# Two products' copies put ahead of both exponentials, and a third product given another bank

## The chip, the cores and the metric

The kernel runs on one core of a Trainium2 chip. Five engines of that core work side by side, each through its own instructions in order: TensorE (PE, matrix products; its weight loads are listed apart as PEld), VectorE (DVE), ScalarE (ACT), GpSimd (POOL) and SyncE (SP), which here only starts transfers. They wait for one another through semaphores. Matrix products land in PSUM, an accumulator memory that is used here as eight banks of 128 partitions by 512 floats; the other engines copy from there to SBUF, the main on-chip memory. The metric is device time in microseconds, lower is better.

## The reference

A batch of attention heads, where each query row keeps only its 32 highest scores, is followed by a two-layer network with an exact GELU:

```python
scores = (q @ k.T) / sqrt(64)                # 8 batches, 8 heads, 576 rows of 64
kth = 32nd largest score of each row
attn = softmax(where(scores >= kth, scores, -1e9))
x = (attn @ v), heads side by side           # 4608 rows of 512
h = x @ w_in                                 # 512 -> 2048
g = 0.5 * h * (1 + erf(h / sqrt(2)))
out = g @ w_out                              # 2048 -> 512
```

All of it is in 32-bit floats.

## The kernel before, in words

The attention is cut into 144 items, 18 for each batch. A main item is a pair of heads and a tile of 128 query rows; the last 64 query rows of a batch (row tile `NM`) make two more items, each with two pairs of heads. In an even batch the sixteen main items come first and the two of the last rows after them, in an odd batch the other way round. Two batches make a ring of 36 items (`RINGS`), and "item 5 of a ring" means an item whose number is 5 modulo 36. Main items come in twos, and the product with the values is done at the odd one of the two, for both.

One pass of the main loop, number n, works on several items at once: scores of item n+2 (`scores`, and `last_keys` for their last keys), the 32 highest of item n (`top_k` on DVE, helped by sums on POOL), threshold and exponentials of item n-1 (`threshold` on POOL; `select` and `softmax` on ACT), the transposes of item n-2 (`transposes`), and the product of item n-3 (`attend`). Between these the loop puts pieces of the two-layer network, `mlp(1)`, so that PE has work. The order written in the loop is the order on each engine; no planner changes it.

`softmax(n - 1, e)` issues the exponential of one of two heads on ACT and adds up its denominators. From these, POOL (`add_small`, line 547) and DVE (`inverse`, the reciprocal of line 541) make the factor with which POOL normalises the row (line 589). The GELU and the exponential need different tables of ACT, so a pass has table loads.

Some items are transposed in another way: DVE turns blocks of 32 by 32 (`square_p`), SP writes them to DRAM (`write_p`, line 632) and reads them back turned into the tile `pt` (`read_p`, line 642). For those the product comes a pass later. `moved(i)` says so of main items: items 3, 5, 13, 23, 25 and 31 of a ring (`LATER`), from item 36 on and only below 136. `delayed(i)` says so of items of the last query rows: 16, 18 and 19 of a ring. Their product is not done at the usual place of the pass, but in `mids`, which calls `attend`, then copies the product into `xT` (`copy_x`), the input of the network, and then starts the next reads into `pt`.

Where in an odd pass `mids` stands is set here (`room` counts network pieces, `mid` lists products to do, `starts_next` holds the second item of each batch, among them item 19 of a ring):

```python
if mid and (mid[0] in starts_next or mid[0] % RINGS == LATER[0]):
    mlp(1); mids()
softmax(n - 1, 0)
if mid:
    mlp(1); mids()
if n % 2 and ahead_of_x:
    softmax(n - 1, 1)
```

`LATER[0]` is 3. So for item 3 and for item 19 the product and its copy are issued ahead of both exponentials, for the other moved items between the two, or behind the first where the second comes later in the pass.

PSUM is shared out by tags. From pass 13 on (`few`), `bank(name)` always gives the one bank `z`: it serves the product `seven` of the network (`seven_piece`, copied out as `p` at line 1003), the small transposes `tp_t` with the last keys of a later item (copied out at 381 and 677), and products `o` that are not moved. `pair_tile(name)` gives the two banks `pr`: for the scores `s_ps` (copied out at 416), for the transposes `tp` (lines 688 and 703), and for a moved item's product `o`, which takes one of the two. In an even pass the scores of two items are made, the first of them in the two banks `l1`, which also hold the network's first layer `h_ps`. A new user of a tag waits until the last one has been copied out.

Of the kernel before, what the change touches and what calls it, by code (L numbers as in the profile page):

```python
# [14 lines left out]
def kernel(  # L15
# [76 lines left out]
    def raw_of(n, pair):  # L92
        if n != "v":
            return raws[n][pair % 2 if pair < SQUARES else 0]
        return raws[n][pair % len(raws[n])]
# [7 lines left out]
    def issue(f):  # L103

        if held[0]:
            late_issues.append(f)
        else:
            f()
# [8 lines left out]
    def load(n, pair, queue=None, queue2=None):  # L117
        if pair >= n_pairs:
            return
        queue = queue or nc.sync  # L120
        queue2 = queue2 or queue
        b, h0 = pair // NP, 2 * (pair % NP)
        src = sources[n]
        if n != "v" and pair >= SQUARES:
            t = flat[n][0]
            for e in range(2):
                at = e * TL if n == "k" else 0
                for d in range(2):
                    rows, cols = slice((2 * e + d) * SQ, (2 * e + d + 1) * SQ), slice(d * SQ, (d + 1) * SQ)
                    queue.dma_start(  # L130
                        out=t[rows, at : at + S].rearrange("i (c j) -> i c j", j=SQ),
                        in_=src[b, h0 + e, :, cols].rearrange("(c i) j -> i c j", i=SQ),
                    )
            return
        t = raw_of(n, pair)
        for e in range(2):

            end = TL if pair >= SQUARES and e == 0 else S
            main = end % S
            queue.dma_start(  # L140
                out=t[:, 0:NM, e, :], in_=src[b, h0 + e, main : main + SM].rearrange("(t p) d -> p t d", p=P)
            )
            rows = slice(0, TL) if n == "q" else slice(e * TL, (e + 1) * TL)
            queue2.dma_start(out=t[rows, NM, e, :], in_=src[b, h0 + e, end - TL : end])
# [121 lines left out]
    def place_of(b, row):  # L266

        if row < SM:
            return b // 2 * RING + b % 2 * (SM + 2 * TL) + row
        return b // 2 * RING + SM + b % 2 * TL + row - SM  # L270
# [9 lines left out]
    def bank(name):  # L280

        tag = "z" if few[0] else ("z", "y0", "y1", "y2")[turn[0] % 4]
        turn[0] += 1
        return ps.tile([P, 512], f32, tag=tag, bufs=1, name=name)
# [75 lines left out]
    def half(r, e):  # L360


        return slice((r ^ e) * TL, ((r ^ e) + 1) * TL)

    def pair_tile(name, tag="pr"):
        return ps.tile([P, 2, 512], f32, tag=tag, bufs=1, name=name)
# [114 lines left out]
    def smaller(i):  # L481

        if paired(i):
            both, top = lists_of[i][:, :, 1].bitcast(i32), lists_of[i][:, :, 0].bitcast(i32)
            nc.gpsimd.tensor_tensor(into_of(i)[:, :, 1].bitcast(i32), both, top, op=ALU.subtract)  # L485
# [73 lines left out]
    def softmax(i, e):  # L559

        if i < 0 or i >= N:
            return
        st, s = stat_of[i], row(i, e)
        if (i, e) not in selected:
            select(i, e)
        nc.scalar.activation(  # L566
            s, s, func=AF.Exp, bias=st["bias"][:, e : e + 1], scale=1.0,
            accum_out=st["den"][:, e : e + 1],
        )
# [23 lines left out]
    def squared(i):  # L593

        if not SINGLE.stop - 2 < i < N - 2:
            return False
        if items[i][1] == NM:
            return i % RINGS != RINGS // 2 - 1
        return moved(i) or (i % 2 == 0 and i % RINGS != 12)

    LATE = (15, 17, 19, 23)
    LATER = (3, 5, 13, 23, 25, 31)

    def moved(i):

        return RINGS <= i < N - 8 and i % RINGS in LATER

    def delayed(i):

        return squared(i) and items[i][1] == NM  # L610
# [4 lines left out]
    RINGS = 2 * len(items) // B  # L615
# [114 lines left out]
    shared = []  # L730

    def column(tok):

        at = tok % RING
        return at if at < COLS else at - COLS

    def attend(i):

        if i < 0 or i >= N:
            return False  # L740
        pair, t = items[i]
        b, at = divmod(pair, NP)
        if t < NM and t % 2 == 0:
            return False
        pt = pt_now[0]
        both = t == NM and delayed(i - 1) and not delayed(i)
        alone = t < NM or not delayed(i) or delayed(i ^ 1)
        o = shared.pop() if both else pair_tile("o")[:, 0] if moved(i) else bank("o")
        off = 2 * TL if both else 0
        n, row = (2 * P, (t - 1) * P) if t < NM else (TL, SM)  # L750
        tok = place_of(b, row)
        gap = RING if t == NM else COLS if tok % RING >= COLS else RING - COLS
        assert read[0] >= tok - gap + n
        c = slice(column(tok), column(tok) + n)
        if t < NM:
            vt = raw_of("v", pair)
            for j in range(NJ):
                for e in range(2):
                    nc.tensor.matmul(  # L759
                        o[e * D : (e + 1) * D, 0:n], lhsT=vt[:, j, e, :],  # L760
                        rhs=pt[:, e * NJ + j if j < NM else NM, :],
                        start=(j == 0), stop=(j == NJ - 1),
                    )
            copies.append(lambda: nc.scalar.copy(out=xT[:, at, c], in_=o[:, 0:n]))
        else:
            for r in range(2):
                vt = raw_of("v", pair + r)
                for j in range(NJ):
                    for e in range(2):
                        nc.tensor.matmul(  # L770
                            o[e * D : (e + 1) * D, off + r * TL : off + (r + 1) * TL],
                            lhsT=vt[:, j, e, :],
                            rhs=pt[:, e * NJ + j if j < NM else NM, i % 2 * P :][:, half(r, e)],
                            start=(j == 0), stop=(j == NJ - 1),
                        )
            if not alone:
                shared.append(o)
            else:
                first = 0 if both else at
                copies.append(lambda: nc.scalar.copy(  # L780
                    out=xT[:, first : at + 2, c],
                    in_=o[:, 0 : off + 2 * TL].rearrange("p (r n) -> p r n", n=TL),
                ))

        if t == (NM if b % 2 == 0 else NM - 1):
            for r in range(2 if t == NM else 1):
                f = lambda r=r: load("v", pair + r + NP)
                if delayed(i) or moved(i):
                    soon.insert(0, f)
                elif both and r:  # L790
                    later.append(f)
                else:
                    issue(f)
        if at == (NP - 1 if t < NM else NP - 2):
            assert n_tok[0] == tok
            n_tok[0] = tok + n
        return True
# [333 lines left out]
    def mlp(n):  # L1131
        for _ in range(n):
            if done[0] >= len(pieces) or pieces[done[0]][0] > ready[0] or left[0] == 0:
                return
            pieces[done[0]][1]()
            done[0] += 1
            left[0] -= 1
            if eager[0]:
                run_gelus()
                run_small(9)  # L1140
# [69 lines left out]
    starts_next = [x + 1 for x in starts]  # L1210
    sums_in = {START + 8 + j: j for j in range(FT // 2)}
    ahead = N + 4
    for n in range(ahead):

        held[0] = n < N and squared(n - 2)
        mid = [i for i in (n - 5, n - 4) if delayed(i) and n % 2 and (i % 2 or i in starts)]
        if moved(n - 4):
            mid = [n - 4]
# [9 lines left out]
        def mids():  # L1228
            attend(mid.pop(0))
            if not mid:  # L1230
                copy_x()
                read_p(n - 3)
                issue_soon()
# [66 lines left out]
            softmax(n - 1, 1)  # L1300
        if few[0]:
            room = ODD if n % 2 else 0
            if mid and (mid[0] in starts_next or mid[0] % RINGS == LATER[0]):
                mlp(1)
                mids()
                room -= 1
            if n % 2 or not ahead_of_x:
                softmax(n - 1, 0)
            if mid:
                mlp(1)  # L1310
                mids()
                room -= 1
            if n % 2 and ahead_of_x:
                softmax(n - 1, 1)
            mlp(room)
# [24 lines left out]
        if n > 0:  # L1340
            smaller(n + 1)
        late_exps = RINGS < n < N - 1 and n % RINGS in LATE
        if not late_exps:
# [93 lines left out]
```

## Time and profile before

| | |
|---|---|
| median of 3 runs | 1458.59 us (1458.47 to 1459.49) |
| the profiled execution's own time | 1461.52 us |
| its span, first to last instruction | 1459.6 us |
| mean granted clock of TensorE | 0.999 |
| ACT busy, with its share of the span | 1050.2 us, 72% |
| POOL busy | 1131.3 us, 78% |

The rows in the prediction are of three kinds. A row of waits gives the engine and line that waited, the engine, tile and line it waited for, and then the total, the number of times and the longest, in microseconds. A row of the order of time gives the start in microseconds from the start of the span, the duration, the engine, the line, the operation, the tile written and the tiles read, the shapes, and how many such instructions are put together; in brackets stands how long the engine was idle before it and what ended that. A row of a window gives its bounds, its length, and the busy time of PE, PEld, DVE, ACT and POOL in it with their numbers of instructions, then the clock, the share of the DMA engines and the rate of transfers. Ends of matmuls are modelled, because TensorE works on several at once.

### The profile page before, as it was taken

How to read it: one execution, taken by the hardware profiler on the slowest of the kernel's cores; microseconds unless marked ns; L12 is line 12 of the kernel's file. 1: busy time of each engine (PE TensorE's matmuls, PEld its weight loads, DVE VectorE, ACT ScalarE, POOL GpSimd, SP SyncE). 2: the span in 40 equal slices, each digit the busy share in tenths (PEclk: the TensorE clock that was granted, in tenths of full speed). 3: DMA queues.
4: the chain of work that ended last, by engine and by line, in shares of the span. 5: the costliest groups of instructions: out<-in, count | busy, mean ns of one | idle time of the engine just before them, and what ended most of it. 6: DMA issues, size and time to landing. Idle time of an engine off the chain costs nothing. (4 is left out here: it accounts for less than half of the span.)

```text
span 1459.6 us, 26560 instructions
## 1 busy us (share of the span) xinstructions
PE 1439.8 (99%) x8567; PEld 1121.3 (77%) x8567; DVE 1324.4 (91%) x3345; ACT 1050.2 (72%) x1871; POOL 1131.3 (78%) x1290
## 2 busy tenths in 40 slices
PE   8999999999999999999999999999999999999999
PEld 6776578877777778787777778778777777787887
DVE  8999899999999999999999999999999999999701
ACT  7999977767768776777776777777676767677620
POOL 6787657887798878887898878886888887878632
PEclk9999999999999999999999999999999999999999
DMA  7524310045465446556646365556556443664200
GB/s 199 147 87 119 91 48 1 9 100 100 92 135 97 83 90 145 106 121 130 121 88 129 64 121 105 128 115 128 115 104 138 90 80 78 133 125 92 50 15 15
DMA packets 627147, 143.57 MB, mean 98 GB/s; under 512 B 532768, under 2 KB 618560, under 8 KB 627008
## 3 DMA queue, kind: packets, MB, share of 16 engines
q1 hardware_dynamic: 625744, 141.45, 46.1%
q8 instruction: 68, 1.11, 0.3%
q14 instruction: 71, 0.58, 0.1%
q10 hardware_dynamic: 1200, 0.39, 0.1%
q0 software_dynamic: 64, 0.03, 0.0%
HBM read 88.73 MB, written 53.08 MB: 97 GB/s over the span
## 5 line engine op out<-in xcount | busy, mean ns | idle before, releaser
L828 PE MATMUL h_ps<-xT,w_in_sb 128*128 128x256 f32 (+1 forms) x2560 | 532.6, 361 | 0.0
L828 PEld LDWEIGHTS h_ps<-xT,w_in_sb 128*128 128x128 f32 x2560 | 439.6, 191 | 67.3 <-issue 10.9
L511 DVE MAX8 top<-lists 128x8 f32<-128x576 f32 (+1 forms) x792 | 474.8, 638 | 0.0
L589 POOL TENSOR_TENSOR s<-s,stat 128x1152 f32<-128x1152 f32 x135 | 311.2, 2305 | 30.9 <-DVE stat L541 29.9
L554 ACT ACTIVATE s<-s,stat 128x576 f32<-128x576 f32 x288 | 217.7, 778 | 127.1 <-POOL stat L534 126.9
L514 DVE MATCH_REPLACE8 lists<-top,lists 128x288 f32<-128x288 f32 (+1 forms) x528 | 307.4, 587 | 0.0
L566 ACT ACTIVATE s<-s,stat 128x576 f32<-128x576 f32 x288 | 224.0, 781 | 7.8
L477 POOL TENSOR_TENSOR lists<-s 128x576 int32<-128x576 int32 x133 | 189.5, 1425 | 0.0
L485 POOL TENSOR_TENSOR lists<-lists 128x576 int32<-128x576 int32 x132 | 186.1, 1410 | 3.1
L759 PE MATMUL o<-pt,raw_v 128*64 128x256 f32 x1280 | 153.0, 384 | 1.9 <-DMA pt<-turned 1.3
L416 ACT ACTIVATE s<-s_ps 128x1024 f32<-128x1024 f32 x127 | 124.8, 1030 | 32.6 <-PE s_ps L408 32.4
L759 PEld LDWEIGHTS o<-pt,raw_v 128*64 128x64 f32 x1280 | 87.3, 137 | 78.9 <-issue 34.4
L984 PE MATMUL y_ps<-w_out_sb,sum 128*128 128x256 f32 x472 | 140.5, 379 | 0.0
L547 POOL TENSOR_SCALAR stat<-stat 128x2 f32<-128x2 f32 x144 | 31.3, 217 | 136.1 <-ACT s L566 129.3
L408 PE MATMUL s_ps<-kt,qm 64*128 64x512 f32 x512 | 129.9, 620 | 0.8 <-ACT s L414 0.8
L844 ACT ACTIVATE g<-h_ps 128x512 f32<-128x512 f32 x144 | 78.2, 595 | 70.6 <-PE h_ps L828 70.1
L984 PE MATMUL y_ps<-w_out_sb,g 128*128 128x256 f32 x480 | 118.0, 383 | 0.0
L514 DVE MATCH_REPLACE8 lists<-first,lists 128x288 f32<-128x288 f32 x264 | 113.9, 436 | 0.0
L526 DVE MAX8 first<-lists 128x8 f32<-128x288 f32 x268 | 106.9, 438 | 0.0
L446 DVE TENSOR_TENSOR lists<-s 128x576 f32<-128x576 f32 x133 | 103.9, 781 | 2.1 <-ACT s L381 2.0
L984 PEld LDWEIGHTS y_ps<-w_out_sb,g 128*128 128x128 f32 x480 | 90.0, 190 | 16.9 <-issue 5.4
L622 DVE STREAM_TRANSPOSE s<-s 128x1152 f32<-128x1152 f32 x74 | 100.8, 1363 | 0.0
(162 smaller groups left out, 2315.6 us busy)
## 6 DMA issues: line engine op xcount, KB each, us to landing
turned<-s SPq DMA_DIRECT2D x296, 144.0 KB, 3.5
pt<-turned SPq DMA_DIRECT2D x296, 144.0 KB, 3.2
raw_v<-in_v_dram SPq DMA_DIRECT2D x64, 128.0 KB, 2.8
raw_q<-in_q_dram SPq DMA_DIRECT2D x112, 72.0 KB, 2.4
raw_k<-in_k_dram SPq DMA_DIRECT2D x112, 72.0 KB, 2.4
out_dram<-y SPq DMA_DIRECT2D x30, 256.0 KB, 3.5
w_out_sb<-in_moe_w_in_dram SPq DMA_DIRECT2D x14, 511.8 KB, 4.9
w_out_sb<-in_moe_w_out_dram SPq DMA_DIRECT2D x10, 511.8 KB, 4.1
```

The lines of the kernel that those rows point to most:

```text
L408: nc.tensor.matmul(s_ps[:, e], lhsT=q_t[rows, :], rhs=kt[rows, main_keys(pair)], start=True, stop=True)
L416: nc.scalar.activation(spread(s, S + TL, SM), s_ps, func=AF.Copy, scale=scale)
L477: nc.gpsimd.tensor_tensor(t[:, :, 1].bitcast(i32), a.bitcast(i32), b.bitcast(i32), op=ALU.add)
L485: nc.gpsimd.tensor_tensor(into_of(i)[:, :, 1].bitcast(i32), both, top, op=ALU.subtract)
L511: nc.vector.max(x[:, e], src[:, e])
L514: nc.vector.match_replace(dst[:, e], x[:, e], src[:, e], LOWEST)
L554: nc.scalar.activation(s, s, func=AF.Prelu, bias=st["neg"][:, e : e + 1], scale=1.0, alpha=STEEP)
L566: nc.scalar.activation(s, s, func=AF.Exp, bias=st["bias"][:, e : e + 1], scale=1.0, accum_out=st["den"][:, e : e + 1],)
L589: nc.gpsimd.tensor_tensor(s, s, wide, op=ALU.mult)
L759: nc.tensor.matmul(o[e * D : (e + 1) * D, 0:n], lhsT=vt[:, j, e, :], rhs=pt[:, e * NJ + j if j < NM else NM, :], start=(j == 0), stop=(j = ...
L828: nc.tensor.matmul(h_tile(u)[:, i, :], lhsT=w_in_sb[:, ko, f * P : (f + 1) * P], rhs=xT[:, ko, c0 : c0 + n], start=(ko == 0), stop=(ko == ...
L984: nc.tensor.matmul(acc[names][:, k], lhsT=lhsT, rhs=rhs, start=(j == 0 and k == 0), stop=(j == FT // 2 - 1 and k == 1),)
```

## The change

Two things are changed. The list of items whose product and copy are issued ahead of both exponentials grows from item 3 to items 3, 5 and 31 of a ring. By `moved`, this concerns items 41, 77 and 113, and items 67 and 103. And the product of item 19 of a ring, the last one of the last query rows (items 55, 91 and 127), takes one of the two banks `pr` in place of the bank `z`. `attend(18)`, just before it, keeps `z`. Nothing is computed differently.

```diff
     LATE = (15, 17, 19, 23)
+    COPY_FIRST = (3, 5, 31)
     LATER = (3, 5, 13, 23, 25, 31)
...
         alone = t < NM or not delayed(i) or delayed(i ^ 1)
-        o = shared.pop() if both else pair_tile("o")[:, 0] if moved(i) else bank("o")
+        aside = moved(i) or delayed(i) and i in starts_next
+        o = shared.pop() if both else pair_tile("o")[:, 0] if aside else bank("o")
...
             room = ODD if n % 2 else 0
-            if mid and (mid[0] in starts_next or mid[0] % RINGS == LATER[0]):
+            if mid and (mid[0] in starts_next or mid[0] % RINGS in COPY_FIRST):
                 mlp(1)
                 mids()
                 room -= 1
```

## The prediction

> **What bounds the kernel now.** I read the shares of the engines first, then what TensorE (PE) and VectorE (DVE) waited for, then the order of time around the three kinds of place that the change touches.
>
> ```profile
> span 1459.6 us, 26560 instructions
> ...
> PE 1439.8 (99%) x8567; PEld 1121.3 (77%) x8567; DVE 1324.4 (91%) x3345; ACT 1050.2 (72%) x1871; POOL 1131.3 (78%) x1290
> ```
>
> ```profile
> PE tp L688 <- ACT xT L764: 3.5, 4, 1.0
> ...
> PE o L759 <- DMA pt<-turned: 1.3, 1, 1.3
> ...
> PE o L770 <- ACT p L1003: 0.8, 3, 0.3
> ```
>
> ```profile
> DVE stat L541 <- POOL stat L547: 51.8, 54, 6.2
> ```
>
> ```profile
> 592.00:724.00 132.00, 131.90 (x752) 103.22 (x751) 129.71 (x328) 94.55 (x169) 105.12 (x118) 1.00 0.62 121
> ```
>
> The first view says that PE is busy for 99% of the span and DVE for 91%. The second (total, times, longest, in us) names nearly all that PE loses once the start is over: the transposes `tp` wait four times for the copy into `xT`, and the product `o` waits three times for the copy `p` out of the bank `seven`. Those seven waits, 4.3 us, are the whole prize. The third row shows that DVE waits for PE's side of the kernel too: 54 times for a GpSimd (POOL) result. The last row (length, then busy PE, weight loads, DVE, ACT, POOL) shows a stretch in which both are full: 131.9 and 129.7 of 132 us. So a microsecond given to PE counts only if DVE can follow, and I look for that at each place.
>
> The Trainium skill, "Perfetto Trace Analysis", section "Identifying the Most-Contended Engine", would have TensorE judged by its weight loads and not by matmul busy time; by that PE stands at 77%, DVE at 91% is the bound, and filling PE's gaps brings nothing. The rows bear on it so: 1121.3 us over 8567 loads is 0.13 us each, while four `seven` matmuls in the next fence take 0.215 us each from start to start (436.60 to 437.46), so a stretch without a gap shows loads well under 100% too. The kinds differ, so the trace does not settle it; a time in which PE's gaps bring nothing is the second rival.
>
> **The change part by part.** (a) Item 5 of a ring, three places (items 41, 77, 113). PE's, ACT's, POOL's and DVE's order of time at the first:
>
> ```profile
> 436.60 1.03 PE L982 MATMUL seven<-w_sum,g 128*128 128x256 f32 x4
> 437.46 1.03 PE L984 MATMUL y_ps<-w_out_sb,g 128*128 128x256 f32 x4
> 438.42 2.38 PE L759 MATMUL o<-pt,raw_v 128*64 128x256 f32 x20
> ...
> 443.45 0.59 PE L984 MATMUL y_ps<-w_out_sb,sum 128*128 128x256 f32 x2
> 445.02 1.09 PE L688 MATMUL tp<-ident,s 128*128 128x128 f32 x8 [0.97 <-ACT xT L764]
> ...
> 446.91 1.99 PE L408 MATMUL s_ps<-kt,qm 64*128 64x512 f32 x8
> 448.83 1.52 PE L759 MATMUL o<-pt,raw_v 128*64 128x256 f32 x12
> ```
>
> ```profile
> 442.15 0.38 ACT L1003 COPY p<-seven 128x256 f32<-128x256 f32 x1
> 442.55 1.28 ACT L566 ACT_TABLE_LOAD   x1
> 443.84 0.78 ACT L566 ACTIVATE s<-s,stat 128x576 f32<-128x576 f32 x1
> ...
> 444.62 0.35 ACT L764 COPY xT<-o 128x256 f32<-128x256 f32 x1
> 444.87 0.78 ACT L566 ACTIVATE s<-s,stat 128x576 f32<-128x576 f32 x1
> ...
> 445.64 0.26 ACT L381 ACTIVATE s<-tp_t 128x128 f32<-128x128 f32 x1
> 445.80 0.26 ACT L677 COPY pt<-tp_t 128x128 f32<-128x128 f32 x1
> 446.15 1.01 ACT L703 COPY pt<-tp 128x1024 f32<-128x1024 f32 x1
> ```
>
> ```profile
> 452.35 0.73 POOL L865 TENSOR_TENSOR sum<-g 128x256 f32<-128x256 f32 x1 [1.33 <-PE y_ps L984]
> ...
> 457.38 0.22 POOL L547 TENSOR_SCALAR stat<-stat 128x2 f32<-128x2 f32 x1
> ```
>
> ```profile
> 456.11 0.79 DVE L526 MAX8 first<-lists 128x8 f32<-128x288 f32 x2
> 457.63 0.17 DVE L541 RECIPROCAL stat<-stat 128x2 f32<-128x2 f32 x1 [0.74 <-POOL stat L547]
> ```
>
> The product `o` lies in the transposes' banks and ended at 438.42 + 2.38 = 440.80; its copy stood behind the table load (1.28) and the first exponential (0.78) and began at 444.62. Ahead of both it begins when L1003 ends, at 442.53, and is done by 442.88. PE's last matmul before the transposes ends at 444.04, so they start 0.97 earlier. On ACT nothing is added: the copy takes 0.25 (444.62 to 444.87) on either side of the exponential, the first exponential comes 0.25 later, the second, which ends the sums that POOL waits for, stays at 444.87. PE's order of work is the same, SP's and POOL's too: the multilayer piece and the `pt` read follow the product as before.
>
> What is late next: `pt<-tp` (L703) cannot start before L677 ends, 445.80 + 0.26 = 446.06, and holds the banks to 447.07. The second half of the scores `s_ps` needs them: the eight matmuls run from 446.91 to 448.83, 0.96 for half, so 0.97 earlier the half would start at 446.90. With some 0.05 for the signal (copy end 444.97 to transposes 445.02) it waits about 0.22: 0.75 is left. DVE's limit is the same by accident: POOL's run from 452.35 to 457.38 starts when PE has read the old sums, moves with PE, and DVE is ready at 456.90 against 457.63. I take 0.74 a place, 2.2 in all. Bounds: nothing (DVE or a DMA takes it) to 0.97 a place, 2.9.
>
> (b) Item 19, the last product of the last query rows, three places (55, 91, 127), first one:
>
> ```profile
> 574.78 1.39 PE L770 MATMUL o<-pt,raw_v 128*64 128x64 f32 x40 [0.26 <-ACT p L1003]
> ...
> 579.12 1.04 PE L688 MATMUL tp<-ident,s 128*128 128x128 f32 x8
> ```
>
> ```profile
> 576.24 0.27 ACT L780 COPY xT<-o 128x128 f32<-128x128 f32 x1 [1.51 <-PE o L770]
> ```
>
> ```profile
> 592.10 0.17 DVE L541 RECIPROCAL stat<-stat 128x2 f32<-128x2 f32 x1 [0.32 <-POOL stat L547]
> ```
>
> In the transposes' banks it no longer waits for `seven` to be copied out of the shared bank: 0.26 off. ACT stood idle 1.51 for this product, so its whole following chain moves with it. The new holder costs nothing: the next user of the banks is `tp` at 579.12 and the copy ends at 576.51, 2.6 before. DVE's wait of 0.32 at 592.10 lets 0.26 through. Matmul ends are modelled, so the true gap may be larger; DVE would pass 0.32 of it. I take 0.26 a place, 0.8 in all, bounds 0 and 1.0. Zero is the case where the next `pt` read sets the pace: PE waited 1.3 for one once.
>
> (c) Item 31, two places (67, 103; item 139 is past the last moved one):
>
> ```profile
> 687.38 2.38 PE L759 MATMUL o<-pt,raw_v 128*64 128x256 f32 x20
> ...
> 688.89 0.38 ACT L1003 COPY p<-seven 128x256 f32<-128x256 f32 x1
> ...
> 692.38 0.26 ACT L381 ACTIVATE s<-tp_t 128x128 f32<-128x128 f32 x1
> ...
> 692.57 0.22 POOL L547 TENSOR_SCALAR stat<-stat 128x2 f32<-128x2 f32 x1 [1.32 <-ACT s L566]
> 693.53 0.22 POOL L534 TENSOR_SCALAR stat<-top 128x2 f32<-128x2 f32 x1 [0.74 <-DVE top L511]
> ...
> 1035.25 1.09 PE L688 MATMUL tp<-ident,s 128*128 128x128 f32 x8 [0.53 <-ACT xT L764]
> 1066.67 0.17 DVE L541 RECIPROCAL stat<-stat 128x2 f32<-128x2 f32 x1 [1.14 <-POOL stat L547]
> ```
>
> At 67 there is no wait of PE to remove, and a wait is added: ACT is ready for the copy at 689.27, the product ends at 689.76, so ACT stands 0.49 with the table load, both exponentials and two copies behind it. The cover: POOL's sum L547 moves from 692.57 to 693.06, and POOL's next instruction waits for DVE until 693.53 anyway. Cost 0; without that cover it would be up to 0.5. At 103 PE's 0.53 goes, and DVE's next wait, 1.14, lets it through: 0.53. It may be less in a run where PE was not late there (the 1.3 us DMA wait stands before it in the same ring).
>
> Sum: 2.2 + 0.8 + 0.5 = 3.5 on the profiled execution, whose own time is 1461.5, its span 1459.6; it lies 2.9 above the median of 1458.6. Since (c) may be a loss of that execution alone, the timed runs should gain 3.0 to 3.5: 1458.6 - 3.3 = 1455.3.
>
> **The rivals.** *More.* If the banks are free in time and DVE follows fully: 3 x 0.97 + 3 x 0.32 + 0.53 = 4.4, time 1454.2. For it: the stalls repeat exactly and everything after them shifts alike. Against: 446.06 and 457.63 above both stop at 0.74.
>
> *It is taken back.* PE's gaps go, but DVE or the `pt` reads keep their times, as in the full stretch from 592 to 724; the second half of the ring absorbs it. Gain 0 to 0.8, time about 1458.2. For it: DVE's 129.71 of 132. Against: DVE waits before and after that stretch (0.74, 0.32, 1.14) for what PE delivers.
>
> *Slower.* DVE's L446 and POOL's L589 follow the same reciprocal, and once in the trace they met:
>
> ```profile
> 446.94 0.73 DVE L446 TENSOR_TENSOR lists<-s 128x576 f32<-128x576 f32 x1
> ...
> 1007.78 2.11 POOL L589 TENSOR_TENSOR s<-s,stat 128x1152 f32<-128x1152 f32 x1
> 1008.08 2.42 DVE L446 TENSOR_TENSOR lists<-s 128x576 f32<-128x576 f32 x1 [0.51 <-ACT s L381]
> ```
>
> There L446 waited 0.51 for ACT's L381, started behind L589 and took 2.42 for 0.73: 1.69 lost. If the reordered ACT queue makes L381 late at the five moved places, that is 8.4 against 3.5 gained: 1463.5. It decides when L381 ends after DVE reaches L446: 445.90 against 446.94 at item 5, which the change does not delay, and 692.64 + 0.49 = 693.13 at item 67, where DVE cannot start it before POOL's 693.53. Over 0.4 us of margin at all five, so unlikely. The Trainium skill, "SBUF - State Buffer", "Who interferes with whom", says that a DVE instruction with two SBUF inputs is blocked for a whole GpSimd instruction that reads SBUF; the 2.42 beside 2.11 agrees.
>
> **How the numbers follow.** Forecast 0.49 (its own range 1454.6 to 1456.2), more 0.20, taken back 0.24, slower 0.07. A measurement of this kernel tells about 0.2%, 2.9 us, from no change: faster means below 1455.7. Three quarters of the forecast and all of "more" lie there, 0.57; the rest of the forecast and "taken back" are no change, 0.36; slower 0.07. The range 1453.6 to 1458.6 takes in the first two and most of the third.
>
> **What would show it.** Right: in PE's waits `tp` for `xT` and `o` L770 for `p` are gone, scores L408 for `pt` L703 stand there with about 0.2 three times; ACT's copy lies ahead of the table load and waits 0.5 for PE at item 67; DVE's wait for L547 shrinks by about 3 us. Wrong: PE's waits gone but as much idle time in new rows (`pt<-turned`, h_ps, L703 with more than 0.7 each), or L446 with over 2 us at a changed place.

## The result and the profile after

The changed kernel takes 1455.88 us (median of 16 runs, 1455.24 to 1457.15) against 1458.72 (1458.40 to 1460.01), a ratio of 0.998 with a 95% interval of 0.9972 to 0.9987: 2.84 us less, where 3.3 were forecast. That is 0.19%, clear of the runs' spread and just on the no-change side of the 0.2% that the prediction had drawn. The profiled execution took 1455.84 us with a span of 1453.9.

What TensorE waits for in the changed kernel (total, times, longest), first its row of shares:

```profile
PE 1439.0 (99%) x8567; PEld 1117.4 (77%) x8567; DVE 1322.6 (91%) x3345; ACT 1049.8 (72%) x1871; POOL 1131.5 (78%) x1290
```

```profile
PE s_ps L408 <- ACT pt L704: 0.5, 3, 0.2
...
PE o L772 <- DMA pt<-turned: 0.3, 1, 0.3
```

The four waits of the transposes for `xT` and the three of the product for `p` are gone. In their stead stand three waits of the scores for the copy L704 (L703 before), 0.5 in all, and one for a read into `pt`. The shares hardly moved: they were no measure of what could be had. DVE's wait for POOL, 51.8 us before, is

```profile
DVE stat L541 <- POOL stat L547: 47.4, 48, 6.2
```

4.4 less, where about 3 was given as a sign.

At item 5, first place, in the order of time of PE, ACT and DVE:

```profile
441.86 0.59 PE L986 MATMUL y_ps<-w_out_sb,sum 128*128 128x256 f32 x2
442.30 1.04 PE L689 MATMUL tp<-ident,s 128*128 128x128 f32 x8
...
444.13 1.13 PE L408 MATMUL s_ps<-kt,qm 64*128 64x512 f32 x4
445.44 1.13 PE L408 MATMUL s_ps<-kt,qm 64*128 64x512 f32 x4 [0.18 <-ACT pt L704]
446.49 2.38 PE L761 MATMUL o<-pt,raw_v 128*64 128x256 f32 x20
```

```profile
440.56 0.38 ACT L1005 COPY p<-seven 128x256 f32<-128x256 f32 x1
440.81 0.41 ACT L766 COPY xT<-o 128x256 f32<-128x256 f32 x1
441.24 1.28 ACT L566 ACT_TABLE_LOAD   x1
442.53 0.78 ACT L566 ACTIVATE s<-s,stat 128x576 f32<-128x576 f32 x1
```

```profile
455.31 0.17 DVE L541 RECIPROCAL stat<-stat 128x2 f32<-128x2 f32 x1
...
795.63 0.17 DVE L541 RECIPROCAL stat<-stat 128x2 f32<-128x2 f32 x1
```

The copy now lies ahead of the table load, the transposes follow PE's last matmul at once, and half of the scores then waits 0.18 for the banks (0.22 was forecast). DVE's reciprocal, which had waited 0.74 in this place, does not wait any more. The last two rows are the same instruction in two rings, so their distance is the length of a ring: 340.32 us. The same pair before was

```profile
799.05 0.17 DVE L541 RECIPROCAL stat<-stat 128x2 f32<-128x2 f32 x1 [0.74 <-POOL stat L547]
```

and the row at 457.63 that the prediction shows: 341.42. A ring is 1.10 shorter. How much of that is item 19's place, the same instruction shows right behind it, in the changed kernel and, for the first row, before:

```profile
580.45 0.17 DVE L541 RECIPROCAL stat<-stat 128x2 f32<-128x2 f32 x1 [0.94 <-POOL stat L547]
...
589.43 0.17 DVE L541 RECIPROCAL stat<-stat 128x2 f32<-128x2 f32 x1 [0.32 <-POOL stat L547]
```

```profile
583.12 0.17 DVE L541 RECIPROCAL stat<-stat 128x2 f32<-128x2 f32 x1 [1.31 <-POOL stat L547]
```

From 455.31 to 589.43 are 134.12, and before from 457.63 to 592.10, the row in the prediction, 134.47: 0.35 for item 19, and about 0.74 for item 5. The wait behind item 19 that became shorter is the first one, 1.31 to 0.94. The one of 0.32 that the prediction took for DVE's limit is still 0.32.

At item 31, place 67, the wait that the change adds, and what hid it (ACT, then POOL):

```profile
687.11 0.37 ACT L766 COPY xT<-o 128x256 f32<-128x256 f32 x1 [0.53 <-PE o L761]
```

```profile
690.51 0.22 POOL L547 TENSOR_SCALAR stat<-stat 128x2 f32<-128x2 f32 x1 [1.96 <-ACT s L566]
690.83 0.22 POOL L534 TENSOR_SCALAR stat<-top 128x2 f32<-128x2 f32 x1
```

ACT waits 0.53 for the product (0.49 forecast). POOL's L534, which had waited 0.74 for DVE, now waits for nothing: the cover was nearly used up, but held.

The two profiles are 5.7 us apart, twice what the runs show. Two parts of that are not the change. The `seven` matmuls before the first changed place stand at 436.60 in the one and here in the other:

```profile
435.00 1.03 PE L984 MATMUL seven<-w_sum,g 128*128 128x256 f32 x4
```

1.6 us earlier ahead of anything that differs; in all other profiles here, too, the work at this place stands 1.4 to 1.7 earlier than in the profile before. And the ring in which the first profile has PE's 1.3 us wait for a read takes 342.59 there (799.05 to 1141.64) and 340.29 here (795.63 to 1135.92), 1.2 more than a ring without that wait differs by. What is left, 2.9, fits the change. That the profile after has no such wait is an accident of the execution as far as the record shows: in the seven other profiles of kernels that read what they should, the same product waits 0.8 to 1.4.

### The profile page after: what moved, and what is told of

The parts are those of the page before. It is cut to its first block, busy times and chain, and to the rows that moved or that the text cites. A ratio compares the mean times of both kernels' runs of the same rounds, so it can differ in the third digit from the quotient of the medians.

```text
span 1453.9 us, 26560 instructions
## 1 busy us (share of the span) xinstructions
PE 1439.0 (99%) x8567; PEld 1117.4 (77%) x8567; DVE 1322.6 (91%) x3345; ACT 1049.8 (72%) x1871; POOL 1131.5 (78%) x1290
## 5 line engine op out<-in xcount | busy, mean ns | idle before, releaser
L589 POOL TENSOR_TENSOR s<-s,stat 128x1152 f32<-128x1152 f32 x135 | 311.6, 2309 | 30.6 <-DVE stat L541 29.9
L446 DVE TENSOR_TENSOR lists<-s 128x576 f32<-128x576 f32 x133 | 102.2, 769 | 1.7 <-ACT s L381 1.5
```

What stands on the lines that cost most here:

```text
L589: nc.gpsimd.tensor_tensor(s, s, wide, op=ALU.mult)
```

## The experiments

Each kernel ran beside the kernel before on the same chip; a difference is that of the medians.

**One part at a time.** The first edit leaves item 31 and item 19 as they were:

```diff
-    COPY_FIRST = (3, 5, 31)
+    COPY_FIRST = (3, 5)
...
-        aside = moved(i) or delayed(i) and i in starts_next
+        aside = moved(i)
```

> Item 5 alone is put ahead of both exponentials (item 31 and item 19 as before). Theory (DVE's reciprocal and the banks of the transposes stop the gain at about 0.74 us a place): 3 x 0.74 = 2.2 us less than before, some 1456.5; PE's wait of the transposes for xT is gone at the three places, and the scores wait about 0.2 for L703's copy in its stead. Rival 'more' (nothing stops it): 2.9 us less, some 1455.8. Rival 'taken back' (the full stretch of DVE absorbs it): 0 to 0.5 us less.

1456.99 against 1459.20: 2.21 us less (ratio 0.9984, 0.9975 to 0.9993). In its profile the reciprocal stands in two rings at

```profile
455.21 0.17 DVE L541 RECIPROCAL stat<-stat 128x2 f32<-128x2 f32 x1
...
795.89 0.17 DVE L541 RECIPROCAL stat<-stat 128x2 f32<-128x2 f32 x1
```

340.68 apart, 0.74 less than before, and three times 0.74 is 2.22. The theory holds. "Taken back" falls by the time, whose interval runs from 1.0 to 3.6 us less; "more" (0.97 a place) lies inside it and falls by the ring alone.

The second edit changes the bank of item 19's product alone:

```diff
-    COPY_FIRST = (3, 5, 31)
+    COPY_FIRST = (3,)
```

> Item 19's product alone takes a bank of the transposes. Theory: 0.26 us a place by the wait shown, up to 0.32 by DVE's wait behind it, so 0.8 to 1.0 us less than before, some 1457.8; a place where the next read into pt is late gives less (0.5 us in all). PE's wait of line 770 for the copy p is gone three times. Rival 'taken back': no change, 1458.7.

1459.61 against 1459.20, ratio 1.0003 (0.9994 to 1.0012): nothing, and the theory missed. The runs also spread from 1457.78 to 1461.15, more than those of any other kernel here. Its profile shows that the wait went all the same, and what stands there now: PE's waits for reads, the product of the second of them, and the reciprocal behind item 19 in two rings:

```profile
PE o L761 <- DMA pt<-turned: 1.1, 1, 1.1
...
PE o L772 <- DMA pt<-turned: 0.4, 1, 0.4
```

```profile
1256.68 1.39 PE L772 MATMUL o<-pt,raw_v 128*64 128x64 f32 x40 [0.35 <-DMA pt<-turned]
```

```profile
581.14 0.17 DVE L541 RECIPROCAL stat<-stat 128x2 f32<-128x2 f32 x1 [0.91 <-POOL stat L547]
...
922.27 0.17 DVE L541 RECIPROCAL stat<-stat 128x2 f32<-128x2 f32 x1 [1.04 <-POOL stat L547]
```

Here the ring takes 341.13, and before it took 341.42 (583.12 to 924.54), so 0.29 was won in that ring. Place by place, from the reciprocal behind item 5 to the second one behind item 19, the three rings take 134.13, 134.13 and 134.55 (456.00 to 590.13, 797.13 to 931.26, 1139.46 to 1274.01), and before 134.47, 134.48 and 134.46: 0.34 and 0.35 were won and then nothing. At the third place the row at 1256.68 tells why: item 19's own product, which had waited 0.26 for `p`, now waits 0.35 for its own read into `pt`.

The next read is close behind as well. PE comes sooner to a product whose read through DRAM does not come sooner. In the profile before, that read (line 642) landed 1.45 and 0.30 us before the product after item 19 began in the first and third ring; in the second PE already stood 1.3 us for it, and stands 1.1 here. That became the next theory, tested below. It does not explain all: this profiled execution won 0.6 at the three places, and why the median shows none of it can't be read from one execution.

The third edit puts item 31 alone ahead:

```diff
-    COPY_FIRST = (3, 5, 31)
+    COPY_FIRST = (3, 31)
...
-        aside = moved(i) or delayed(i) and i in starts_next
+        aside = moved(i)
```

> Item 31 alone is put ahead of both exponentials (two places). Theory: no change within 0.3 us, 1458.7: at item 67 the added wait of ACT (about 0.5 us) is hidden by POOL's wait for DVE, and at item 103 there is a wait of PE to win only in a run in which the ring was late before. Rival 'the wait at 103 is always there': 0.5 us less. Rival 'the added wait of ACT costs': up to 1.0 us more.

1459.20 against 1459.20, ratio 0.9998 (0.9990 to 1.0007): no difference seen, as the theory had it, though the interval is wide enough to hold the 0.5 of the first rival. Its profile caught an execution in which the second ring was late (the product after item 19 waited 1.36 for its read), and there item 31 did earn something. From the second reciprocal behind item 19 to the one eighteen passes on it takes 169.33 (932.15 to 1101.48). The profile before, late by 1.27, takes 169.95 (933.53 to 1103.48), and the changed kernel, not late, 168.75 (929.74 to 1098.49). So being late costs 1.2 us, and with item 31 ahead about 0.6 of it is won back. Its counterpart is the whole change without item 31 (`COPY_FIRST = (3, 5)`, item 19 in the transposes' banks):

> The whole change without item 31 (the list is 3 and 5; item 19's product in a bank of the transposes). Theory (item 31 is worth nothing): the same as the changed kernel, 2.8 us less than before, within 0.3. Rival 'item 31 earns its 0.5 us where the ring is late': 2.3 less than before.

1456.62 against 1459.18, 2.56 less (ratio 0.9983, 0.9974 to 0.9992). That lies between the two numbers expected, and its runs (1455.89 to 1458.21) overlap those of the change: whether item 31 is worth 0.3 us beside the others stays open. Its profile is late too (1.43), has PE wait 0.4 for `xT` at item 103, and takes 170.02 over the same stretch, as one without item 31 ahead should.

**More copies ahead.** The list is made to hold all moved items:

```diff
-    COPY_FIRST = (3, 5, 31)
+    COPY_FIRST = (3, 5, 13, 23, 25, 31)
```

> On top of the whole change, the moved items 13, 23 and 25 are also put ahead of both exponentials (nine more places). Theory (a copy ahead gains only where PE waits for it, and PE shows no such wait any more): the same as the changed kernel within 0.5 us, some 1455.9, 2.8 less than before. Rival 'ahead is always better': 0.3 us or more a place, below 1453.2. Rival 'ACT standing before the product costs': up to 0.5 us a place, up to 1460.

1456.70 against 1459.20, 2.50 less, ratio 0.9980 (0.9971 to 0.9989): no better than the change. Here a copy put ahead earned where PE stood waiting for it, and nothing that can be measured where it did not. Its profile has more waits for reads than the change's:

```profile
PE o L761 <- DMA pt<-turned: 2.9, 4, 1.4
```

**What stops item 5 at 0.74.** The small copy into `pt` goes behind the large one, so that the banks come free sooner; what `put_off` holds is issued at the end of `both`, behind the large copy:

```diff
+            end = lambda: nc.scalar.copy(out=pt[:, NM, x : x + P], in_=tp[:, at : at + P])
+            if i % RINGS == 7 and moved(i - 2):
+                keys()
+                put_off.append(end)
+                return
...
+            while put_off:
+                put_off.pop(0)()
```

> On top of the whole change, at item 5's three places ACT copies the small transposes into pt (L678) behind the large ones (L704), so that the banks of the transposes come free 0.15 to 0.25 us sooner. Theory (two limits stand at the same height, and DVE's reciprocal is the other): PE's wait of the scores for L704, 0.18 a place, goes, and the time stays as with the change, 2.8 us less than before, within 0.4. Rival 'the banks alone are the limit': 0.2 us more a place, 3.5 less than before.

1456.28 against 1459.12, 2.84 less (ratio 0.9978, 0.9969 to 0.9988): as with the change, though the interval (1.8 to 4.5) holds the rival's 3.5 too. The wait of the scores is gone, in all three places. At the first, DVE's reciprocal stands 18.68 behind the one two passes before it (436.77 to 455.45; with the change 436.54 to 455.31, 18.77), so it came 0.09 sooner at most, and waits for nothing. At the second and third, PE's next product waits for its read:

```profile
787.27 2.38 PE L770 MATMUL o<-pt,raw_v 128*64 128x256 f32 x20 [0.44 <-DMA pt<-turned]
...
1128.40 2.38 PE L770 MATMUL o<-pt,raw_v 128*64 128x256 f32 x20 [0.59 <-DMA pt<-turned]
```

So the time came out as expected, but the reason was incomplete: beside the banks and DVE, the read into `pt` is a third limit. In the changed kernel's profile it landed 0.39 and 0.35 before these two products, more than the 0.18 by which they could have come sooner; here it also landed later. The profiled execution is the slowest of the ten (1457.44), so how often this limit is the lowest stays open.

**The rival "slower", made to happen.** On top of the change, at item 5's places the copy of the last keys (L381) is put last, behind five copies of the small piece:

```diff
+            if i % RINGS == 7 and moved(i - 2):
+                put_off.extend([end] * 5 + [keys])
+                return
```

> On top of the whole change, at item 5's three places ACT's copy of the last keys (L381) is put behind the copies into pt, and the small copy into pt is made five times, so that the keys come about 0.6 us after DVE is ready for L446. What is computed stays the same. Theory (the rival 'slower' has a true mechanism): L446 then starts behind POOL's L589 and takes over 2 us in place of 0.73, DVE loses about 2 us a place and has nothing to spare there: 5 to 6 us more than with the change, 2.5 to 3.5 us more than before. Rival 'no blocking': L446 takes its 0.73 us and only the 0.6 of waiting is lost, 1.8 us more than with the change, 1 us less than before.

1460.78 against 1459.12, ratio 1.0011 (1.0003 to 1.0020): 1.66 us more than before, and so 4.5 more than the change, which had 2.84 less. DVE and POOL at the first place:

```profile
446.56 1.60 DVE L446 TENSOR_TENSOR lists<-s 128x576 f32<-128x576 f32 x1 [1.20 <-ACT s L381]
```

```profile
445.44 2.11 POOL L589 TENSOR_TENSOR s<-s,stat 128x1152 f32<-128x1152 f32 x1 [0.41 <-DVE stat L541]
```

L446 waited 1.20 (0.6 was meant) and then took 1.60 in place of 0.73: L589 holds until 447.55, and L446 ends 0.61 after that. DVE lost 2.07 a place. Of that 0.66 came back by the second reciprocal behind item 19 (457.31 to 590.77 is 133.46, with the change 134.12), which leaves 1.4 a place; 4.5 over three is 1.5. The mechanism is seen in the row, and "no blocking", by which L446 keeps its 0.73, falls by it. The time alone would not decide, since the wait was twice what was meant and PE's next product also waited 0.41 for L381, here and at the second place; and the price was set too high, at 5 to 6. The Trainium skill, "SBUF - State Buffer", "Who interferes with whom", says that a DVE instruction with two SBUF inputs contends with a GpSimd instruction that reads SBUF, over ports that it calls an exclusive lock; the rows agree, L446 ending 0.61 after L589 did.

**Why item 19 alone brought nothing.** Two kernels share a base in which items 19 and 20 of a ring read a tile that has landed long ago:

```diff
-            d = turned.pop(i)
+            d = new = turned.pop(i)
+            if i % RINGS in (19, 20):
+                d = read_last[0]
+            read_last[0] = new
```

> The kernel before, but items 19 and 20 of a ring read into pt the tile of the item before them, which has landed in DRAM long ago; the weights of those items are so the wrong ones. It is the base for the next run. The read that follows the last product of the last query rows then waits only for PE to be done with pt, and lands 0.7 us or more sooner. Theory: PE's 1.3 us wait for pt goes, and with it what follows from it in that ring; 0 to 1 us less than before.

> The same base as the run beside it (items 19 and 20 read the tile of the item before), with item 19's product in a bank of the transposes. Theory (item 19 alone brought nothing because the next read into pt, through DRAM, did not come sooner): with that read out of the way, 0.8 to 1.0 us less than its base. Rival 'PE's 0.26 is absorbed elsewhere': no difference to its base within 0.4 us.

The base took 1458.66 (1458.33 to 1459.16), 0.46 less than before, with an interval that takes in no change (ratio 0.9996, 0.9988 to 1.0005). In its profile the read after item 19's product lands 2.16, 1.62 and 1.58 us before the product that needs it. With item 19's product moved it took 1458.02 (1457.51 to 1458.32), 0.64 less than the base; no run of one lies within the runs of the other. The reciprocal in the base, and then with item 19 moved:

```profile
581.46 0.17 DVE L541 RECIPROCAL stat<-stat 128x2 f32<-128x2 f32 x1 [1.25 <-POOL stat L547]
...
922.91 0.17 DVE L541 RECIPROCAL stat<-stat 128x2 f32<-128x2 f32 x1 [1.40 <-POOL stat L547]
```

```profile
581.32 0.17 DVE L541 RECIPROCAL stat<-stat 128x2 f32<-128x2 f32 x1 [0.93 <-POOL stat L547]
...
922.46 0.17 DVE L541 RECIPROCAL stat<-stat 128x2 f32<-128x2 f32 x1 [1.04 <-POOL stat L547]
```

341.45 and 341.14: 0.31 a ring, and DVE's waits in these rows are shorter by 0.32 and 0.36. With that read out of the way the gain is there, somewhat smaller than the 0.8 to 1.0 expected; the rival "absorbed elsewhere" falls. Only the next read was out of the way: item 19's own read still held its product for 0.70 at the third place in the base's profile. The whole change on that base:

> The whole change, and items 19 and 20 of a ring read the tile of the item before them, as in the two runs on that base (wrong weights for those items). Theory (item 5's part and item 19's part add up once the read is out of the way): base 0.46 below before, item 5 another 2.2, item 19 another 0.6 to 1.0, together 3.3 to 3.7 us less than before. Rival 'item 5's own reads become the limit': no more than with the change, 2.8 less.

1455.99 against 1459.18, 3.19 less (ratio 0.9978, 0.9969 to 0.9987), a little under the 3.3 to 3.7 expected. The 0.46 of the base, 2.21 of item 5 and 0.64 of item 19 make 3.31, so the parts' medians add up to the whole within about 0.1. The interval (1.9 to 4.5) does not part this from the rival's 2.8, and its profile shows some of the rival: at item 5's third place the product waits 0.27 for its read, and at item 19's third place 0.30.

## Why the prediction was right, step by step

*What bounds the kernel.* Right. Filling seven gaps of PE moved the time by two thirds of what they summed to (2.84 of 4.3). That filling PE's gaps would bring nothing, since PE's weight loads stand at 77%, does not hold here: item 5's part alone gained 2.21 with the loads at that share.

*(a) Item 5.* Right: 0.74 a place and 2.2 in all, 2.21 measured, the wait of the scores 0.18 for 0.22. The ring, 0.74 shorter, bears out the size; that the timed 2.21 agrees to the hundredth is luck, with an interval from 1.0 to 3.6. That DVE's reciprocal was one stop fits its wait falling from 0.74 to nothing. The prediction named two stops; the fifth experiment showed a third, the read into `pt`.

*(b) Item 19.* The wait named was the right one and it went; the size did not hold, and one reading was wrong. Forecast 0.8; alone it measured 0.4 slower with an interval around no change, on top of item 5 0.35 less (2.56 less 2.21, two kernels on two chips), with the next read out of the way 0.64 less. The step that failed is "I take 0.26 a place", for all three: the profiles of this part alone and of the whole change show 0.34 to 0.37 at the first two places and nothing at the third, where item 19's own read then holds its product. The case set aside as the lower end, "where the next `pt` read sets the pace", was nearer than it was made: the next read had already held PE in the second ring. And DVE's wait of 0.32 at 592.10 is no bound: it is 0.32 with and without the change, and the wait that passes the gain on is the one of 1.31 at 583.12.

*(c) Item 31.* Forecast 0.5 in the profile and half of that in the runs; measured 0.0 alone, 0.3 less beside the others, neither apart from nothing. PE's 0.53 belongs to executions in which a read has held PE before, as the text suspected: it stands in the profiles that are late there (0.4 to 0.8 without item 31 ahead) and not in those of the base. The added ACT wait was free, as worked out.

*The sum.* 3.3 forecast, 2.84 measured. The medians split it into 2.21 for item 5, 0.35 for item 19 and 0.28 for item 31, which would put nearly all of the shortfall on (b); with intervals of 1.3 either way that split is not shown. "More" fell at item 5's two stops. "Taken back" was right in kind for item 19 only, and by a read, not by the full stretch of DVE. "Slower" did not occur, and its mechanism was seen by making it.

## What to carry to other kernels

A stall on a saturated engine is worth what the next waiter leaves over: for each gap look up the next user of the same bank, the other engine's wait behind it, and the landing of the next transfer, and take the smallest. Where one execution is profiled, measure the same instruction a period apart; the length of a period without a rare wait in it is steadier than the whole span, which here differed by twice the change's worth. A copy moved ahead earns only where someone stands waiting for it. Before a wait is taken for the limit of a gain, check that it is the first one behind the gap: here the next one, of 0.32, never moved.

## What the runs showed that was not expected

The reads through DRAM are a hidden bound. They hardly show in the waits (1.3 us once in the profile before). Yet when PE was made earlier, waits for them came up that were not there before: 0.4 with item 19 alone at its own product, and with all copies ahead 2.9 over four places, of which 1.4 stands where the 1.3 stood. Giving two of the reads in each ring a tile that had landed long ago brought 0.46 us at the median, which is not clear of no change, but it narrowed the runs: 11 of them spread over 0.8 us, against 2.8 for 32 of the kernel before beside them. With item 19 moved they spread over 3.4 us, and over 0.8 with those early tiles. So much of the spread is an accident of when transfers land; what makes a read land late was not looked into.
